# A cached attention kernel: V in one buffer, K in two, and loops of one unit

## The chip, the cores and the metric

The kernel runs on one core of a Trainium2 chip. TensorE (PE), VectorE (DVE), ScalarE (ACT), GpSimd (POOL) and SyncE (SP) each work through an instruction list of their own and wait for each other by semaphores. SP issues all loads; 16 DMA engines carry them out. The metric is the device time of one execution in microseconds. The version before takes 1937.41 us, the median of 3 runs (1937.18 to 1937.42).

## The reference

Two independent attention blocks, A and B, are computed and their outputs put side by side:

```python
def _A_ref(x, k_cache, v_cache, wq, wo):       # B's is the same
    q = (x @ wq).reshape(B, Sq, Hq, Dh).transpose(0, 2, 1, 3)
    scores = jnp.einsum("bhqd,bhkd->bhqk", q, k) * (Dh ** -0.5)
    p = _softmax(scores, axis=-1)
    o = jnp.einsum("bhqk,bhkd->bhqd", p, v)
    return o.transpose(0, 2, 1, 3).reshape(B, Sq, Hq * Dh) @ wo
```

The batch is 2, there is one query row, 32 heads, 8192 cached positions, a head size of 192, and a model size of 640. All is bf16. The caches K and V are by far the largest inputs: each of the four is 2 x 32 x 8192 x 192 numbers, some 201 MB. Every number of them is used once.

## The kernel before

**Units.** A unit u is two neighbouring heads of one batch entry of one block: 64 units, 0 to 63. Its K is one load of 6144 KB, its V another; 128 partitions hold the two heads' positions, 64 partitions for each head and 128 positions for each partition. First the queries are made from x and wq and stand in `qall`, spread over the partitions.

**One unit, step by step.** The names are those of the keys in the code, and the prediction uses them too.
- m(u,c), c = 0 to 3: VectorE multiplies a quarter of K(u) with the query into one of two `prod` buffers (`dve_mul`).
- s(u,c): TensorE adds up the 192 products of a position to 16 partial sums, by 12 matmuls with the identity, into a PSUM bank `scps` (`pe_sum`). m(u,c+2) needs s(u,c) done, as there are two `prod` buffers.
- r(u,c): VectorE adds up the 16 partial sums into `sc` (`dve_red`).
- mx(u): VectorE takes the maximum in each partition (`dve_max`); AR(u): GpSimd takes it over all partitions with a partition all-reduce (`pool_ar`).
- nb(u), exp(u): ScalarE scales the maximum and takes the exponential of `sc` into `pb`, with the sums in `rs` (`act_nb`, `act_exp`).
- l(u), pv(u): TensorE adds up `rs` and multiplies `pb` with V(u) by 64 matmuls into a PSUM bank `ops` (`pe_l`, `pe_pv`).
- rc, oh, os(u): VectorE takes the reciprocal of the sum and adds the two halves of the result; of(u): ScalarE scales and stores it.

At the end the results are turned by small matmuls (`pe_turn`), and multiplied with wo (`pe_out`), which is loaded in pieces into buffers that have come free.

**Buffers and loads.** Three buffers of 128 partitions x 24576 numbers rotate over the sequence K0, K1, V0, K2, V1, K3, V2 and so on, whichever kind a load is. Load number i waits until what load i - 3 brought has been used:

```python
return ("m", u, NCH - 1) if kind == "k" else ("pv", u)   # done(i - 3)
```

So V(u) takes the buffer of K(u), after m(u,3), and K(u+1) that of V(u-2), after pv(u-2). `sc`, `mp`, `mg`, `nb`, `rs`, `rc`, `pb` and `ops` exist three times, `scps` three times.

**Order.** The order of each engine's instructions is written out by hand: `put(engine, slot, order, ...)` sorts by slot and then by order within it. VectorE, in slot u: m0, m1, r0, m2, r1, m3, r2, r3, mx, and then rc, oh, os of unit u-2. TensorE: s0, s1, s2, s3 and then l and pv of unit u-1. ScalarE: nb, exp, and of(u-2). `_Stream` finds a stretch that repeats and makes a loop of it; the loops of VectorE, ScalarE and TensorE hold three units, and SP and GpSimd have none. Unit 0 is an exception: m(1,0) stands in slot 0, ahead of r(0,3) and mx(0).

**The end.** SP issues A's whole wo after s(63,3), 29 rows of B's after pv(62), and the last 19 rows in four pieces after pv(63). A row here is 160 KB.

Of the kernel before, what the change touches and what calls it, by code (L numbers as in the profile page):

```python
# [12 lines left out]
class _Stream:  # L13
    virtual = set()

    def __init__(self, name, sem, reg, first=3):
# [101 lines left out]
def build_kernel(nc, blocks, out):  # L118
# [28 lines left out]
    with ExitStack() as es:  # L147
# [4 lines left out]
        rc = [sb(f"rc{i}", [2, 1], F32) for i in range(3)]  # L152
# [4 lines left out]
        pb = [sb(f"pb{i}", [128, 2 * T], BF16) for i in range(3)]  # L157
        actd = sb("actd", [128, 2], F32)
        xw = sb("xw", [128, NBLK * DC * 128 + D], BF16)
        sc = [sb(f"sc{i}", [128, T], F32) for i in range(3)]  # L160
        mp = [sb(f"mp{i}", [128, 2], F32) for i in range(3)]
        mg = [sb(f"mg{i}", [128, 2], F32) for i in range(3)]
        nb = [sb(f"nb{i}", [128, 1], F32) for i in range(3)]
        rs = [sb(f"rs{i}", [128, 2], F32) for i in range(3)]
# [7 lines left out]
        ops = [ps(f"ops{i}", [128, 512], F32) for i in range(3)]  # L172
        scps = [ps(f"scps{i}", [128, TC, DG], F32) for i in range(3)]
# [3 lines left out]
        oacc = [outps[:], qbank[(LASTU * NCH + 1) % 3]]  # L177
        qps = qbank + [outps[:]]
# [16 lines left out]
        S_pe = _Stream("pe", sem("s_pe"), reg, 1)  # L195
# [24 lines left out]
        bk, b62, b63 = buf["k", LASTU], buf["v", LASTU - 1], buf["v", LASTU]  # L220
        assert (bk, b62, b63) == (2, 0, 1)
        woA, wo0, wo1 = bk * BUFE, b62 * BUFE, b63 * BUFE
        pieces = []
        for blk, rows, off, w in ((0, (WR,), woA, [("s", LASTU, NCH - 1)]), (1, (29,), wo0, [("pv", LASTU - 1)]),
                                  (1, (11, 5, 2, 1), wo1, [("pv", LASTU)])):
            r = 29 if off == wo1 else 0
            for n in rows:
                pieces.append((blk, r, r + n, off, w))
                off, r, w = off + n * D, r + n, []
            assert r == (29 if off == wo0 + 29 * D else WR)  # L230
        NA = 0
        assert 29 * D <= BUFE and woA + WR * D <= NBUF * BUFE + 2 * PRODE
# [21 lines left out]
        def ld_wo(n):  # L254
            blk, r0, r1, off, _ = pieces[n]
            src = blocks[blk]["wo"].rearrange("(p i) n -> p (i n)", i=WR)
            return dma(big[:, off:off + (r1 - r0) * D], src[:, r0 * D:r1 * D], ("wo", n))

        def ld_kv(kind, u):
            hp, b = u // B, u % B  # L260
            blk, h = hp // PPB, 2 * (hp % PPB)
            src = blocks[blk][kind][b, h:h + 2].rearrange("s (p t) d -> (s p) t d", p=64)
            return dma(kv[buf[kind, u]], src, (kind, u))

        def pool_ar(u):
            return lambda eng: eng.partition_all_reduce(mg[u % 3][:], mp[u % 3][:], 128, bass.bass_isa.ReduceOp.max)  # L266
# [21 lines left out]
        def dve_red(u, c):  # L288
            return lambda eng: eng.tensor_reduce(sc[u % 3][:, c * TC:(c + 1) * TC], scps[(u * NCH + c) % 3][:], AXL.X, ALU.add)  # L289

        def dve_max(u):
            def fn(eng):
                for s in range(2):
                    r = slice(64 * s, 64 * s + 64)
                    ins = eng.tensor_reduce(mp[u % 3][r, s:s + 1], sc[u % 3][r, :], AXL.X, ALU.max)  # L295
                return ins
            return fn

        def dve_rc(u):
            return lambda eng: eng.reciprocal(rc[u % 3][:], ops[u % 3][0:2, QW:QW + 1])  # L300

        def dve_ohi(u):
            return lambda eng: eng.tensor_copy(o_hi[:], ops[u % 3][32:34, Dh:QW])  # L303

        def dve_osum(u):
            return lambda eng: eng.tensor_tensor(o_sum[:], ops[u % 3][0:2, 0:Dh], o_hi[:], ALU.add)  # L306

        def act_of(u):
            return lambda eng: eng.activation(qall[0:2, S_act.at(u), :], o_sum[:].unsqueeze(1), ACTF.Identity, scale=rc[u % 3][:])  # L309

        def act_nb(u):
            def fn(eng):
                for s in range(2):
                    r = slice(64 * s, 64 * s + 64)
                    ins = eng.activation(nb[u % 3][r, :], mg[u % 3][r, s:s + 1], ACTF.Identity, scale=-scale)  # L315
# [3 lines left out]
        def act_exp(u):  # L319
            def fn(eng):  # L320
                for s in range(2):
                    r = slice(64 * s, 64 * s + 64)
                    dst = pb[u % 3][r, :].rearrange("p (g a j s) -> p g a j s", a=2, j=JB, s=2)[:, :, :, :, s]
                    ins = eng.activation(dst, sc[u % 3][r, :].rearrange("p (g j a) -> p g a j", j=JB, a=2),  # L324
                                         ACTF.Exp, bias=nb[u % 3][r, :], scale=scale, accum_out=rs[u % 3][r, s:s + 1])
# [33 lines left out]
        def pe_sum(u, c):  # L359
            def fn(eng):  # L360
                for j in range(NJ):
                    ins = eng.matmul(scps[(u * NCH + c) % 3][:], ident[:], prod[c % 2][:, :, j * DG:(j + 1) * DG],  # L362
# [4 lines left out]
        def pe_l(u):  # L367
            return lambda eng: eng.matmul(ops[u % 3][0:2, QW:QW + 1], rs[u % 3][:], ones[:], start=True, stop=True)  # L368

        def pe_pv(u):  # L370
            vv = kv[buf["v", u]].rearrange("p (j a) d -> p j (a d)", a=2)

            def fn(eng):
                for j in range(TJ):
                    j0s = 4 * JB * (j // JB) + 2 * (j % JB)
                    ins = eng.matmul(ops[u % 3][0:MP, 0:QW], pb[u % 3][:, j0s:j0s + MP], vv[:, j, :],  # L376
# [20 lines left out]
        def pe_out(n):  # L397
            blk, r0, r1, off, _ = pieces[n]
            wo = big[:, off:off + (r1 - r0) * D].rearrange("p (i n) -> p i n", n=D)
# [9 lines left out]

        def pe_idle(eng):  # L410
            for i in range(8):
                ins = eng.matmul(ops[(LASTU + 1) % 3][:], ident[:], big[:, woA + 512 * i:woA + 512 * (i + 1)], start=True, stop=True)
            return ins
# [21 lines left out]
        for u in range(NU):  # L435
            for c in range(NCH):
                w = [("k", u), ("pq", NP - 1), ("qa", NP - 1), ("qx", NP - 1), back("s", u, c, 2)]
                slot, order = (0, 9.2) if (u, c) == (1, 0) else (u, 2 + 2 * c)
                put("dve", slot, order, dve_mul(u, c), w, ("m", u, c), ("m", c, u % 3))
                put("dve", u, 5 + 2 * c if c < NCH - 1 else 9.5, dve_red(u, c),  # L440
                    [("s", u, c), key("mx", u - 3), key("exp", u - 3)], ("r", u, c), ("r", c, u % 3))
                put("pe", u, 0.1 * c, pe_sum(u, c),
                    [("m", u, c), ("os", -2) if (u, c) == (1, 0) else None, back("r", u, c, 3), ("id1",), ("qx", NP - 1), ("qa", NP - 1)], ("s", u, c), ("s", c, u % 3))
            put("dve", u, 12, dve_max(u), [("r", u, NCH - 1), key("ar", u - 3), ("init",)], ("mx", u), ("mx", u % 3))
            put("pool", u, 0, pool_ar(u), [("mx", u), key("nb", u - 3)], ("ar", u), ("ar", u % 3))
            put("act", u, 0, act_nb(u), [("ar", u), key("exp", u - 3)], ("nb", u), ("nb", u % 3))
            put("act", u, 1, act_exp(u), [("nb", u), key("pv", u - 3), key("l", u - 3), ("init",)], ("exp", u), ("exp", u % 3))
            w0 = [("exp", u), key("os", u - 3), key("rc", u - 3), ("init",)]
            pslot = u + 1
            pe_o = 2  # L450
            put("pe", pslot, pe_o, pe_l(u), w0, ("l", u), ("l", u % 3))
            put("pe", pslot, pe_o + 0.1, pe_pv(u), [("v", u)], ("pv", u), ("pv", u % 3, buf["v", u]))
            put("dve", u + 2, 20, dve_rc(u), [("pv", u), key("of", u - 3)], ("rc", u), ("rc", u % 3))
            put("dve", u + 2, 21, dve_ohi(u), [("pv", u), key("os", u - 1)], ("oh", u), ("oh", u % 3))
            put("dve", u + 2, 22, dve_osum(u), [("oh", u), key("of", u - 1)], ("os", u), ("os", u % 3))
            put("act", u + 2, 4, act_of(u), [("os", u), ("rc", u)], ("of", u), ("of", u % 3))
# [11 lines left out]
        put("act", NU, 6, act_ot(0), [("t", 1, HQ - 1)], ("ot", 0))  # L468
        put("act", E2, 6, act_ot(1), [("t", 1, HL)], ("ot", 1))
        for n, p in enumerate(pieces):  # L470
# [3 lines left out]
            put("pe", E2, 0.01 * n if n <= NA else 2 + 0.01 * n, pe_out(n), w, ("f", n))  # L474
        put("pe", E2, 1, pe_idle, [("of", LASTU)], None)
# [3 lines left out]

        def done(i):  # L480
            if i < 0:
                return None
            kind, u = loads[i]
            return ("m", u, NCH - 1) if kind == "k" else ("pv", u)
# [22 lines left out]
        fills = [(mp[i], -3.0e38) for i in range(3)] + [(t[i], 0.0) for i in range(3) for t in (rs, pb)]  # L507
        for n, (t, v) in enumerate(fills):
            S_pool.add((lambda t, v: (lambda eng: eng.memset(t[:], v)))(t, v), sig=("init",) if n == len(fills) - 1 else None)
        for n in range(128 // HP):  # L510
# [10 lines left out]
                              ("r", u, 2), ("r", u, 3), ("mx", u), ("rc", u - 2), ("oh", u - 2), ("os", u - 2)],  # L521
# [90 lines left out]
```

## Time and profile before

| | us |
|---|---|
| median of 3 runs | 1937.41 |
| the profiled execution: span | 1936.0 |
| TensorE busy (matmuls) | 1545.0 (80%) |
| VectorE busy | 1124.0 (58%) |
| ScalarE busy | 142.3 (7%) |
| GpSimd busy | 28.4 (1%) |
| moved by DMA | 836.91 MB at 432 GB/s |

The span runs from the first to the last instruction of the profiled execution; the runs are timed from outside. "Idle before" in a group's row is the time in which the engine had nothing to do ahead of such an instruction, with what ended most of it. A DMA issue is a short row on SP's queue (SPq); "us to landing" counts from the issue until the last of the 16 engines has reported. In a timeline, the first number is the start from the beginning of the span, the second the time from the start to the end of the row; rows of equal kind that follow each other are merged, with their count at the end (x24).

### The profile page before, as it was taken

The numbers are of one execution on the slowest core, as the hardware profiler recorded it, in microseconds if no ns is written. First come the engines' busy times: TensorE is split into PE (matmuls) and PEld (weight loads), VectorE is DVE, ScalarE is ACT, GpSimd is POOL, SyncE is SP. The second block draws the span as 40 slices with busy tenths as digits, with TensorE's granted clock in tenths as the row PEclk, the third lists the DMA queues.
The fourth block names the chain that finished last, engine by engine and source line by source line (L and its number), as shares of the span: only waits on it lengthen the run. The fifth ranks groups of instructions, "written<-read, shape, count | busy, mean of one in ns | idle before, by whom it ended". The sixth has DMA issues, their size and how long they took to land.

```text
span 1936.0 us, 19059 instructions
## 1 busy us (share of the span) xinstructions
PE 1545.0 (80%) x7728; PEld 743.0 (38%) x7729; DVE 1124.0 (58%) x907; ACT 142.3 (7%) x519; POOL 28.4 (1%) x113
## 2 busy tenths in 40 slices
PE   5777878878878878878878878878878878878878
PEld 2333434434434434434434434433433433433434
DVE  4765565565565565565565565565565565565560
ACT  3100000000000000000000000000000000000000
POOL 0000000000000000000000000000000000000000
PEclk9899989988989988989988999999999999999999
DMA  9999999999999999999999999999999999999999
GB/s 419 427 435 436 432 434 438 430 434 437 434 433 434 437 431 435 437 432 433 436 436 431 434 438 429 436 437 432 434 435 436 430 436 438 428 436 437 433 433 391
DMA packets 19610, 836.91 MB, mean 432 GB/s; under 512 B 2184, under 2 KB 2320, under 8 KB 2576
## 3 DMA queue, kind: packets, MB, share of 16 engines
q1 hardware_dynamic: 19600, 836.78, 99.9%
q8 instruction: 6, 0.10, 0.0%
q14 instruction: 4, 0.03, 0.0%
HBM read 836.77 MB, written 0.01 MB: 432 GB/s over the span
## 4 chain that ended last, share of the span: by engine, by line
DMA 49%; PE 31%; DVE 17%; issue 3%; DVEq 0%; SPq 0%; ACT 0%; ACTq 0%
DMA big<-in_B_k_cache_dram 24%; DMA big<-in_A_k_cache_dram 22%; PE ops L376 18%; DVE big L285 15%; PE scps L362 12%; DMA big<-in_B_wq_dram 2%; DVE sc L289 1%; DMA big<-in_B_wo_dram 1%; PE scps L354 0%; PE ops L368 0%; PE outps L354 0%; DVEq L285 0%; DVE qall L275 0%; PE scps L404 0%; PE oTps L390 0%
## 5 line engine op out<-in xcount | busy, mean ns | idle before, releaser
L285 DVE TENSOR_TENSOR big<-big,qall 128x6144 bf16<-128x6144 bf16 x256 | 852.7, 3351 | 490.7 <-DMA big<-in_B_k_cache_dram 260.6
L362 PE MATMUL scps<-big,ident 128*128 128x512 bf16 x3072 | 815.6, 426 | 358.2 <-DVE big L285 355.7
L376 PE MATMUL ops<-big,pb 128*34 128x384 bf16 x4096 | 676.8, 326 | 0.0
L362 PEld LDWEIGHTS scps<-big,ident 128*128 128x128 bf16 x3072 | 314.3, 107 | 852.7 <-DVE big L285 439.2
L376 PEld LDWEIGHTS ops<-big,pb 128*34 128x34 bf16 x4096 | 395.5, 98 | 258.7
L289 DVE TENSOR_REDUCE sc<-scps 128x32 f32<-128x512 f32 x256 | 175.9, 687 | 227.7 <-PE scps L362 227.7
L315 ACT ACTIVATE nb<-mg 64x1 f32<-64x1 f32 x128 | 25.8, 201 | 1707.7 <-POOL mg L266 1706.9
L324 ACT ACTIVATE pb<-sc,nb 64x128 bf16<-64x128 f32 x128 | 55.8, 436 | 7.8
L266 POOL PARTITION_ALL_REDUCE mg<-mp x64 | 25.7, 402 | 1859.1 <-DVE mp L295 1859.1
L295 DVE TENSOR_REDUCE mp<-sc 64x1 f32<-64x128 f32 x128 | 35.9, 280 | 8.3
L309 ACT ACTIVATE qall<-o_sum,rc 2x192 f32 (+1 forms) x64 | 29.0, 453 | 20.7 <-DVE o_sum L306 19.1
L306 DVE TENSOR_TENSOR o_sum<-ops,o_hi 2x192 f32<-2x192 f32 x64 | 22.1, 346 | 7.7
L354 PE MATMUL scps<-big,xw 128*128 x120 | 23.2, 351 | 2.6 <-DVE xw L271 2.2
L324 ACT ACTIVATION_READ_ACCUMULATOR pb<-sc,nb 64x1 f32 x128 | 23.7, 185 | 0.0
L303 DVE COPY o_hi<-ops 2x192 f32<-2x192 f32 x64 | 22.3, 349 | 2.0
L300 DVE RECIPROCAL rc<-ops 2x1 f32<-2x1 f32 x64 | 10.0, 156 | 21.3 <-PE ops L376 19.3
L275 DVE CAST qall<-scps 64x192 f32 x48 | 17.0, 355 | 7.2 <-PE scps L354 5.4
L280 ACT ACTIVATE qall<-scps 64x192 f32 x48 | 15.6, 324 | 30.5 <-DVE qall L275 28.2
L345 PE MATMUL oTps<-ident,xw 4*128 4x4 bf16 x5 | 0.4, 178 | 21.5 <-DMA xw<-in_B_x_dram 21.5
L354 PEld LDWEIGHTS scps<-big,xw 128*128 128x128 bf16 x120 | 12.4, 103 | 12.1 <-issue 5.9
L368 PEld LDWEIGHTS ops<-ones,rs 128*2 128x2 f32 x128 | 5.5, 82 | 26.9 <-issue 26.9
L404 PE MATMUL outps<-big,oT 128*2 128x320 bf16 x96 | 9.2, 369 | 4.6 <-DMA big<-in_A_wo_dram 4.6
(36 smaller groups left out, 67.6 us busy)
## 6 DMA issues: line engine op xcount, KB each, us to landing
big<-in_A_k_cache_dram SPq DMA_DIRECT2D x32, 6144.0 KB, 28.6
big<-in_A_v_cache_dram SPq DMA_DIRECT2D x32, 6144.0 KB, 27.6
big<-in_B_k_cache_dram SPq DMA_DIRECT2D x32, 6144.0 KB, 28.9
big<-in_B_v_cache_dram SPq DMA_DIRECT2D x32, 6144.0 KB, 27.8
big<-in_A_wq_dram SPq DMA_DIRECT2D x1, 7680.0 KB, 21.2
big<-in_B_wq_dram SPq DMA_DIRECT2D x1, 7680.0 KB, 38.2
big<-in_A_wo_dram SPq DMA_DIRECT2D x1, 7680.0 KB, 29.0
big<-in_B_wo_dram SPq DMA_DIRECT2D x1, 4640.0 KB, 29.3
```

What stands on the lines that cost most here:

```text
L266: return lambda eng: eng.partition_all_reduce(mg[u % 3][:], mp[u % 3][:], 128, bass.bass_isa.ReduceOp.max)
L285: return lambda eng: eng.tensor_tensor(prod[c % 2], t[:, c * TC:(c + 1) * TC, :], qall[:, S_dve.at(u), :].broadcast_to([128, TC, Dh]), ALU ...
L289: return lambda eng: eng.tensor_reduce(sc[u % 3][:, c * TC:(c + 1) * TC], scps[(u * NCH + c) % 3][:], AXL.X, ALU.add)
L295: ins = eng.tensor_reduce(mp[u % 3][r, s:s + 1], sc[u % 3][r, :], AXL.X, ALU.max)
L303: return lambda eng: eng.tensor_copy(o_hi[:], ops[u % 3][32:34, Dh:QW])
L306: return lambda eng: eng.tensor_tensor(o_sum[:], ops[u % 3][0:2, 0:Dh], o_hi[:], ALU.add)
L309: return lambda eng: eng.activation(qall[0:2, S_act.at(u), :], o_sum[:].unsqueeze(1), ACTF.Identity, scale=rc[u % 3][:])
L315: ins = eng.activation(nb[u % 3][r, :], mg[u % 3][r, s:s + 1], ACTF.Identity, scale=-scale)
L324: ins = eng.activation(dst, sc[u % 3][r, :].rearrange("p (g j a) -> p g a j", j=JB, a=2), ACTF.Exp, bias=nb[u % 3][r, :], scale=scale, acc ...
L354: ins = eng.matmul(qps[hp % NQ][:, 0:QW], xbc[:, blk, c, :], wq_t[blk][:, c, S_pe.at(off, QW, QW)], start=(c == 0), stop=(c == DC - 1))
L362: ins = eng.matmul(scps[(u * NCH + c) % 3][:], ident[:], prod[c % 2][:, :, j * DG:(j + 1) * DG], start=(j == 0), stop=(j == NJ - 1))
L376: ins = eng.matmul(ops[u % 3][0:MP, 0:QW], pb[u % 3][:, j0s:j0s + MP], vv[:, j, :], start=(j == 0), stop=(j == TJ - 1))
```

## The change

1. Buffers: V has buffer 2 for itself, K alternates between 0 and 1. V(u) waits for pv(u-1), K(u) for m(u-2,3). SP's order stays K(u+1), V(u), K(u+2), V(u+1).
2. `sc`, `mp`, `mg`, `nb`, `rs`, `rc`, `pb` and `ops` exist once; `scps` four times, one bank for each quarter. So r(u,c) waits for exp(u-1), exp(u) for pv(u-1), and l(u) for os(u-1).
3. Order. TensorE: s0, s1, s2, l and pv of unit u-1, and then s3. VectorE: m(u+1,0) of the next unit comes ahead of r(u,3) and mx(u), in every unit, and rc, oh, os(u-1) ahead of that. ScalarE: of(u-1), nb, exp.
4. Loops: one unit on TensorE, ScalarE and GpSimd, two on VectorE and SP.
5. `pool_ar` has a one-element product on GpSimd ahead of the all-reduce. In the built program a library reload stands ahead of each of the two, in every turn of the loop; before, there was one reload, ahead of the first all-reduce.
6. wo: 38 of A's 48 rows are loaded between V(62) and V(63), into K's buffer 0, after m(62,3). The other 10, and 28 of B's, come after m(63,3) and s(63,3), 19 more go into the `prod` buffers, and the last row into `xw`. `pe_idle` is gone.

```diff
-        rc = [sb(f"rc{i}", [2, 1], F32) for i in range(3)]
+        rc = sb("rc", [2, 1], F32)
...
-        ops = [ps(f"ops{i}", [128, 512], F32) for i in range(3)]
-        scps = [ps(f"scps{i}", [128, TC, DG], F32) for i in range(3)]
+        ops = ps("ops", [128, 512], F32)
+        scps = [ps(f"scps{i}", [128, TC, DG], F32) for i in range(NCH)]
...
+        VB = NBUF - 1
...
-            buf[kind, u] = i % NBUF
-            bcount[i % NBUF] += 1
-            reg[(kind, u)] = (bsem[i % NBUF], 16 * bcount[i % NBUF])
+            n = VB if kind == "v" else u % VB
+            buf[kind, u] = n
+            bcount[n] += 1
+            reg[(kind, u)] = (bsem[n], 16 * bcount[n])
...
-        for blk, rows, off, w in ((0, (WR,), woA, [("s", LASTU, NCH - 1)]), (1, (29,), wo0, [("pv", LASTU - 1)]),
-                                  (1, (11, 5, 2, 1), wo1, [("pv", LASTU)])):
+        for blk, rows, t, off, w in ((0, (38, 10), BIG, 0, FREE0), (1, (28,), BIG, WR * D, FREE1),
+                                     (1, (12, 5, 2), BIG, PROD, []), (1, (1,), XW, 0, [])):
...
         def pool_ar(u):
-            return lambda eng: eng.partition_all_reduce(mg[u % 3][:], mp[u % 3][:], 128, bass.bass_isa.ReduceOp.max)
+            def fn(eng):
+                eng.tensor_tensor(pooled[:], ones[:], ones[:], ALU.mult)
+                return eng.partition_all_reduce(mg[:], mp[:], 128, bass.bass_isa.ReduceOp.max)
+            return fn
...
-                slot, order = (0, 9.2) if (u, c) == (1, 0) else (u, 2 + 2 * c)
-                put("dve", slot, order, dve_mul(u, c), w, ("m", u, c), ("m", c, u % 3))
+                put("dve", u if c else u - 1, 2 + 2 * c if c else 9.3, dve_mul(u, c), w, ("m", u, c), ("m", c, u % VB))
                 put("dve", u, 5 + 2 * c if c < NCH - 1 else 9.5, dve_red(u, c),
-                    [("s", u, c), key("mx", u - 3), key("exp", u - 3)], ("r", u, c), ("r", c, u % 3))
-                put("pe", u, 0.1 * c, pe_sum(u, c),
-                    [("m", u, c), ("os", -2) if (u, c) == (1, 0) else None, back("r", u, c, 3), ("id1",), ("qx", NP - 1), ("qa", NP - 1)], ("s", u, c), ("s", c, u % 3))
+                    [("s", u, c), key("exp", u - 1)], ("r", u, c), ("r", c))
+                put("pe", u, 0.1 * c if c < NCH - 1 else 3, pe_sum(u, c),
+                    [("m", u, c), back("r", u, c, NCH), ("id1",), ("qx", NP - 1), ("qa", NP - 1)], ("s", u, c), ("s", c))
...
-            put("dve", u + 2, 20, dve_rc(u), [("pv", u), key("of", u - 3)], ("rc", u), ("rc", u % 3))
+            put("dve", u + 1, 9.20, dve_rc(u), [("pv", u), key("of", u - 1)], ("rc", u), ("rc",))
...
-        for i, (kind, u) in enumerate(loads):
-            w = [done(i - NBUF)]
-            if i in (1, 2):
-                w = [("pq", PPB * i - 1)]
-            S_sp.add(ld_kv(kind, u), waits=w)
-        for n in range(len(pieces)):
+        for kind, u in loads[:-1]:
+            if kind == "k":
+                load(kind, u, [("pq", PPB - 1)] if u == 1 else [key("m", u - VB, NCH - 1)] if u else [])
+            else:
+                load(kind, u, [key("pv", u - 1)] if u else [("pq", NP - 1)])
+        S_sp.add(ld_wo(0), waits=pieces[0][4])
+        load("v", LASTU, [("pv", LASTU - 1)])
+        for n in range(1, len(pieces)):
             S_sp.add(ld_wo(n), waits=pieces[n][4])
```

More of the change, by code (lines that the diff above doesn't have):

```diff
@@ L367, in pe_l @@
         def pe_l(u):
-            return lambda eng: eng.matmul(ops[u % 3][0:2, QW:QW + 1], rs[u % 3][:], ones[:], start=True, stop=True)
+            return lambda eng: eng.matmul(ops[0:2, QW:QW + 1], rs[:], ones[:], start=True, stop=True)
         def pe_pv(u):
@@ L408, in pe_out @@
             return fn
[L410 to L413, printed above, removed]
         NSLOT = NU + 8
@@ L489, in build_kernel, with load @@
         S_sp.add(ld_wq(1))
-        for i, (kind, u) in enumerate(loads):
-            w = [done(i - NBUF)]
-            if i in (1, 2):
-                w = [("pq", PPB * i - 1)]
-            S_sp.add(ld_kv(kind, u), waits=w)
-        for n in range(len(pieces)):
+        def load(kind, u, w):
+            slot = u if kind == "k" else u + 1
+            blk = u // UPB
+            S_sp.add(ld_kv(kind, u), waits=w, tag=(slot, (kind, u % B, blk)))
+        for kind, u in loads[:-1]:
[6 more added lines that the diff above has]
+        for n in range(1, len(pieces)):
             S_sp.add(ld_wo(n), waits=pieces[n][4])
@@ L506, in build_kernel @@
         S_pool.add(lambda eng: eng.memset(ones[:], 1.0))
[L507 removed]
+        fills = [(mp, -3.0e38), (rs, 0.0), (pb, 0.0)]
         for n, (t, v) in enumerate(fills):
```

134 lines of the change are left out of this document (66 added, 68 removed).

## The prediction

> **What bounds the kernel now.** I read the page first: span, DMA queue, groups, issues.
>
> ```profile
> span 1936.0 us, 19059 instructions
> ...
> q1 hardware_dynamic: 19600, 836.78, 99.9%
> ...
> L285 DVE TENSOR_TENSOR big<-big,qall 128x6144 bf16<-128x6144 bf16 x256 | 852.7, 3351 | 490.7 <-DMA big<-in_B_k_cache_dram 260.6
> L362 PE MATMUL scps<-big,ident 128*128 128x512 bf16 x3072 | 815.6, 426 | 358.2 <-DVE big L285 355.7
> ...
> big<-in_A_k_cache_dram SPq DMA_DIRECT2D x32, 6144.0 KB, 28.6
> ...
> big<-in_A_wq_dram SPq DMA_DIRECT2D x1, 7680.0 KB, 21.2
> ```
>
> The queue is busy for 99.9% of the span; VectorE and TensorE wait for loads or for each other. A load takes 28.6 us to land, and the next rows show that moving it takes about half of that. These are the timelines of one unit, by engine: VectorE, TensorE, then SP.
>
> ```profile
> 911.00 6.63 DVE L285 TENSOR_TENSOR big<-big,qall 128x6144 bf16<-128x6144 bf16 x2 [7.96 <-DMA big<-in_A_k_cache_dram]
> 919.75 0.69 DVE L289 TENSOR_REDUCE sc<-scps 128x32 f32<-128x512 f32 x1 [2.13 <-PE scps L362]
> ...
> 940.03 6.63 DVE L285 TENSOR_TENSOR big<-big,qall 128x6144 bf16<-128x6144 bf16 x2 [7.17 <-DMA big<-in_A_k_cache_dram]
> ```
> ```profile
> 914.41 8.30 PE L362 MATMUL scps<-big,ident 128*128 128x512 bf16 x24 [3.21 <-DVE big L285]
> 923.76 2.76 PE L362 MATMUL scps<-big,ident 128*128 128x512 bf16 x12 [1.05 <-DVE big L285]
> 927.63 2.76 PE L362 MATMUL scps<-big,ident 128*128 128x512 bf16 x12 [1.10 <-DVE big L285]
> 930.32 0.19 PE L368 MATMUL ops<-ones,rs 128*2 128x1 f32 x2
> 930.45 10.57 PE L376 MATMUL ops<-big,pb 128*34 128x384 bf16 x64
> 943.44 1.93 PE L362 MATMUL scps<-big,ident 128*128 128x512 bf16 x6 [2.42 <-DVE big L285]
> ```
> ```profile
> 927.60 0.33 SPq L245 DMA_DIRECT2D big<-in_A_v_cache_dram  x1
> 941.05 0.33 SPq L245 DMA_DIRECT2D big<-in_B_k_cache_dram  x1
> ```
>
> K(u) landed at 911.00, K(u+1) at 940.03: 29.03 us for two loads, 14.5 each. V was issued at 927.60, some 12 us before the load ahead of it was through, K at 941.05, with a whole load still ahead. So the queue never runs dry, and a unit costs its bytes, 29.03 us. That reserve of 12 to 14 us is what the change touches. The profiled execution is the span, 1936.0; the median of the runs is 1937.41, so I add 1.4 at the end.
>
> **The change, part by part.** Buffers and SP's order. V(u) now waits for the V product of unit u-1 (pv(u-1)) instead of the last product of unit u (m(u,3), over at 927.58). K(u+2) still waits for m(u,3) only, but stands behind V(u) on SP. So both loads of a unit are issued at the end of pv(u-1), and the reserve is whatever is left between that end and the landing of K(u+1).
>
> TensorE's order: pv(u-1) moves ahead of the fourth sums s(u,3), which gives it 2.7 us (927.63 to 930.32). VectorE's order: m(u+1,0) moves ahead of r(u,3) and the maximum mx(u). So mx(u) now follows the landing of K(u+1). Behind it stand AR(u) on GpSimd, the exponential exp(u), and, since there is one sc, r(u+1,0), which must wait for exp(u). The queue behind r(u+1,0) is m(u+1,2), s(u+1,2), pv(u), and with it V(u+1) and K(u+3). This is the new chain. The old kernel ran its first unit in just this order:
>
> ```profile
> 72.44 3.35 DVE L285 TENSOR_TENSOR big<-big,qall 128x6144 bf16<-128x6144 bf16 x1
> 75.71 0.68 DVE L289 TENSOR_REDUCE sc<-scps 128x32 f32<-128x512 f32 x1
> 76.42 0.57 DVE L295 TENSOR_REDUCE mp<-sc 64x1 f32<-64x128 f32 x2
> 77.03 3.36 DVE L285 TENSOR_TENSOR big<-big,qall 128x6144 bf16<-128x6144 bf16 x1
> ```
>
> GpSimd's rows of that unit and of one later, and the end of ScalarE's exponential:
>
> ```profile
> 77.18 3.42 POOL L266 PARTITION_ALL_REDUCE mg<-mp  x1 [73.94 <-DVE mp L295]
> ...
> 931.91 0.35 POOL L266 PARTITION_ALL_REDUCE mg<-mp  x1 [29.47 <-DVE mp L295]
> ```
> ```profile
> 81.90 0.18 ACT L324 ACTIVATION_READ_ACCUMULATOR pb<-sc,nb 64x1 f32 x1
> ```
>
> Here m(1,0), r(0,3), mx(0), m(1,1) follow each other, and AR took 3.42 us, against 0.35 later, when VectorE has no large product beside it. It ended at 80.60, just after m(1,1) ended at 80.39. Two readings fit: GpSimd is held while the product runs, or the first call after a library load is slow. In the changed kernel both conditions hold in every unit, so either reading charges it.
> The Trainium skill (SBUF — State Buffer, Who interferes with whom) says that a VectorE instruction with two SBUF inputs shuts out a GpSimd instruction that reads SBUF until it ends; by that rule the first reading is the right one, the trace agrees (3.42 beside 0.35), and the sum stays as it is.
>
> From the start of m(u,0), then: to m(u,1), 77.03 - 72.44 = 4.59. To the end of AR(u-1), 80.60 - 77.03 = 3.57. The added one-element GpSimd product: nothing at the least, one AR (0.35) at the most; I take 0.3. AR to the end of exp, 82.08 - 80.60 = 1.48. From r(u,0) to the end of s(u,2), 926.52 - 919.75 = 6.77. To the end of pv, 941.02 - 930.32 = 10.70. Sum 27.41; SP's start 0.03 later: 27.44.
>
> TensorE's clock comes on top, since there is now a pause of about 3.5 us (r(u,0) and m(u,2) after exp) ahead of s(u,2). What such a pause does, by two stretches of stages (PE busy first, granted clock third from the end) and one row of TensorE:
>
> ```profile
> 910.20:913.60 3.40, 1.00 (x7) 0.39 (x4) 2.60 (x1) 0.00 (x0) 0.00 (x0) 1.00 1.03 448
> 913.60:917.00 3.40, 2.59 (x7) 0.94 (x8) 3.40 (x2) 0.00 (x0) 0.00 (x0) 0.50 1.07 463
> ```
> ```profile
> 1842.40 6.83 PE L362 MATMUL scps<-big,ident 128*128 128x512 bf16 x24 [3.53 <-DVE big L285]
> ```
>
> After 3.21 us of pause the granted clock was 0.50, and two sums took 8.30 instead of twice 2.76: 2.8 us lost; after 3.53 us they took 6.83: 1.3 lost. Here the loss falls on s(u,2) and pv, on the chain. Bounds 0 (no stretch that long falls into one clock step) and 2.8; I take 1.7, nearer the lower row, whose pause is like ours. Together 29.1 from m(u,0) to the issue.
>
> The queue's side. How long an issue into a drained queue takes to land beyond its bytes: the first load, 7680 KB, took 21.2; at 14.5 per 6144 KB its bytes are 18.1, so 3.1 over. Two loads: 29.0 + 3.1, and 0.2, my estimate, from a landing to VectorE's start: 32.3. So m(u+2,0) comes 29.1 + 32.3 = 61.4 after m(u,0), 30.7 a unit instead of 29.03. VectorE's own round is shorter: 29.1 and about 1 us for the three small reads of pv, ahead of m(u+1,0), 30.1 in all, so the queue sets the pace.
>
> The run: m(1,0) starts at 72.44 as before; m(3,0) at 72.44 + 61.4 = 133.8; 30 such steps later m(63,0) at 1975.8. Before, m(63,0), the last 36 us (granted clock, DMA share and GB/s at the end of the row) and the last piece of wo:
>
> ```profile
> 1868.01 6.63 DVE L285 TENSOR_TENSOR big<-big,qall 128x6144 bf16<-128x6144 bf16 x2 [8.23 <-DMA big<-in_B_k_cache_dram]
> ```
> ```profile
> 1900.00:1936.00 36.00, 27.25 (x258) 14.81 (x257) 1.81 (x5) 1.56 (x4) 0.00 (x0) 0.91 0.86 370
> ```
> ```profile
> big<-in_B_wo_dram SPq DMA_DIRECT2D x1, 160.0 KB, 23.2
> ```
>
> The end. V(63) is issued at 1975.8 + 29.1 = 2004.9. The 38 rows of A's wo (6080 KB, 14.3 us) stand between V(62) and V(63) and fill the place of a K load, so no further hole. Behind V(63) come 58 rows, 9280 KB, 21.9 us: the last lands at 2004.9 + 3.1 + 14.5 + 21.9 = 2044.4. The old kernel's last piece, issued at about 1910.7, landed 23.2 later, 2.1 before the end: 2046.5, with 1.4 more **2048**. The old end left 14% of 36 us of queue unused, 5 us, so a better order of wo can't be worth more than that.
>
> What I cost at nothing: loop branches of one unit on VectorE, TensorE and ScalarE (on VectorE the loop turns between mx and m(u,1), which waits for nothing else; AR's 3.57 covers it, and if that cover goes, r(u,0) still waits for s(u,0)); K's own two buffers; single rc, nb, rs, ops (their readers end before the next writer in this order); SP's and GpSimd's loops (SP's own work is one row of 0.33 a load); four banks of scps instead of three; wo's last row in xw.
>
> **Not shown: the library load.** In the built program GpSimd gets a library reload ahead of the added product and another ahead of AR, in every unit; before there was one in the whole run, with 73.94 us of idle time after it. The nearest row bounds one: AR after a load took 3.42, without 0.35, so 0 to 3.07, two 0 to 6.14. I take 0, as AR began 77.18 - 76.99 = 0.19 us after mx, and the 3.42 are explained by the product beside it.
>
> **Rivals.** (a) Not slower: AR's 3.42 was once only. Then exp(u-1) is over at 4.59 + 0.1 + 0.3 + 0.35 + 1.48 = 6.8 after m(u,0), r(u,0) waits for s(u,0) or m(u,1) alone (8.1 to 8.75), and the issue comes at 25.6 to 26.25. The round is (25.6 + 32.3) / 2 = 28.95: the bytes still decide. Only the first step costs, m(3,0) at 72.44 + 57.9 = 130.3 instead of 1868.01 - 60 x 29.0 = 128: 1936 + 2 + 1.4 = 1939. It turns at r(u,0) 8.3 after m(u,0); at 8.75 the round is 29.27, 0.24 x 62 = 15 slower. For it: TensorE's pause ahead of s(u,0) shrinks below 3.2, as s(u-1,3) follows pv. Against: 3.42, in just this order.
> (b) The clock holds: without the 1.7 the round is 59.7, m(63,0) at 72.44 + 59.7 x 31 = 1923, the end 68.9 later with V's issue at 27.44: 1993.5. For it: pauses of 1 us (923.76) cost nothing, and clock steps can split a pause; against: all pauses above 2.4 us cost.
> (c) The reloads count 3.07 each. From mx on: 0.1 + 3.07 + 0.3 + 3.07 + 0.35, AR ends 11.45 after m(u,0) instead of 8.46. VectorE's round becomes 30.1 + 3.0 = 33.1, with the full clock loss 34.2: 62 x 4.1 to 62 x 5.2 more, 2195 to 2265. Against it: nothing that the trace shows; it lies in the dark of those 73.94 us.
> The Trainium skill (GPSIMD Engine Reference, Instruction dispatch) gives 5.95 us for loading code at the first call after a reload; by that the estimate is 8.7 us more in the chain and about 2580. No run here shows it, and it is the case that speaks most against this change.
> (d) The reloads cost more than 3.07 each. At twice that, VectorE's round is 33.1 + 6.1 = 39.2 and the time about 2570; for and against as in (c), and against it that AR began 0.19 us after mx.
>
> **How the numbers follow.** The forecast, with 2020 to 2100 about it: 0.38. (b), 1985 to 2019: 0.17. (a): 0.10, of which 0.02 faster (up to 5 us from the end), 0.05 same, 0.03 slightly slower. (c), to 2265: 0.19. (d): 0.16. The range takes in all but (d) and the fastest corner: 1938 to 2265. Within 0.2%, 3.9 us, is what a measurement of this kernel can't tell from no change. Faster 0.02, same 0.05, slower 0.93.
>
> **What will show it.** Right: DMA share clearly below 99.9%; SP waiting for the V product alone; AR's mean near 3.5, or 0.35 after a late added product; r(u,0) waiting for exp, not for sums; m(u,0) every 30.7 us; half clock in s(u,2). Wrong: gaps between mx and AR of several us (reload); a queue still at 99%.

## The result, and the profile after

The changed kernel takes 3209.6 us (median of 4 runs, 3203.4 to 3217.3) beside 1937.3 for the kernel before on the same chip: a ratio of 1.657 (95% interval 1.654 to 1.660). The direction was as predicted, the size was not: 3209.6 lies far above 2048 and above the range's end of 2265. Nearest was rival (d), reloads that cost more than 3.07 us each, and it too was too small at 2570.

From the page of the kernel after: the span, the load queue, the chain that ended last, and four groups (group rows: number, busy time and mean ns of one, then the idle time before them and what ended most of it).

```profile
span 3215.7 us, 20311 instructions
...
q1 hardware_dynamic: 19744, 836.78, 62.4%
...
issue 46%; PE 31%; DVE 20%; ACT 2%; POOL 1%; DVEq 0%; ACTq 0%; POOLq 0%
...
L292 DVE TENSOR_TENSOR big<-big,qall 128x6144 bf16<-128x6144 bf16 x256 | 857.1, 3348 | 3.0 <-ACT qall L287 1.0
...
L296 DVE TENSOR_REDUCE sc<-scps 128x32 f32<-128x512 f32 x256 | 175.4, 685 | 1377.7 <-ACT pb L331 1306.7
...
L271 POOL TENSOR_TENSOR pooled<-ones 128x1 f32<-128x1 f32 x64 | 14.9, 233 | 2471.3 <-issue 2371.3
...
L272 POOL PARTITION_ALL_REDUCE mg<-mp x64 | 23.7, 370 | 672.3 <-issue 672.3
```

The queue is no longer the bound (62.4% where it was 99.9%), and VectorE's products don't wait for K at all (3.0 us in the whole run; 490.7 before). VectorE waits 1306.7 us for exp instead. The all-reduce itself takes 0.37 us, but GpSimd stands idle for 672.3 us ahead of the 64 all-reduces, 10.5 us each, with "issue" as the cause: there is no semaphore that it waits for. That is the library reload. Timeline and groups have no row for it, and its time can only be read as this idle time; where it starts is shown by the short rows MODIFY_POOL_CONFIG of GpSimd's sequencer (POOLq), two for each reload, which the view of a source line lists (count, then ns min/median/max):

```profile
L271 POOLq MODIFY_POOL_CONFIG  x128: 1/11/83, 2.6 to 3148.3; - x128
...
L272 POOLq MODIFY_POOL_CONFIG  x128: 1/1/11, 81.3 to 3173.6; - x128
```

Those for the product stand 0.23 us behind the end of mx (median; in the first and the last unit alone they stand ahead of it), and those for the all-reduce right behind the product. One unit in the timeline (start, duration, engine):

```profile
1538.05 3.34 DVE L292 TENSOR_TENSOR big<-big,qall 128x6144 bf16<-128x6144 bf16 x1
...
1542.10 0.57 DVE L302 TENSOR_REDUCE mp<-sc 64x1 f32<-64x128 f32 x2
...
1554.21 0.18 POOL L271 TENSOR_TENSOR pooled<-ones 128x1 f32<-128x1 f32 x1 [38.07 <-issue]
1565.40 0.37 POOL L272 PARTITION_ALL_REDUCE mg<-mp  x1 [11.01 <-issue]
...
1567.45 0.69 DVE L296 TENSOR_REDUCE sc<-scps 128x32 f32<-128x512 f32 x1 [21.38 <-ACT pb L331]
...
1571.46 5.30 PE L369 MATMUL scps<-big,ident 128*128 128x512 bf16 x12 [22.57 <-DVE big L292]
...
1576.81 10.65 PE L383 MATMUL ops<-big,pb 128*34 128x384 bf16 x64
...
1587.49 0.34 SPq L266 DMA_DIRECT2D big<-in_A_v_cache_dram  x1
...
1588.34 3.33 DVE L292 TENSOR_TENSOR big<-big,qall 128x6144 bf16<-128x6144 bf16 x1
```

mx is over at 1542.67. The product comes 11.5 us later, the all-reduce 11.0 us after that; over the 64 units the means are 11.2 and 10.5. Behind it everything waits in the order that the prediction names: exp, r(u,0), s(u,2), pv. What closes the round is not V's load, though: VectorE has rc, oh and os of pv ahead of the next m(u,0), and starts that at 1588.34, without a wait for K. The unit takes 50.3 us here, 49.3 in the mean.

### The profile page after: what moved, and what is told of

It reads as the page before. It is cut to its first block, busy times and chain, and to the rows that moved or that the text cites. A ratio compares the mean times of both kernels' runs of the same rounds, so it can differ in the third digit from the quotient of the medians.

```text
span 3215.7 us, 20311 instructions
## 1 busy us (share of the span) xinstructions
PE 1565.4 (49%) x7721; PEld 739.3 (23%) x7721; DVE 1123.8 (35%) x907; ACT 141.9 (4%) x519; POOL 40.7 (1%) x171
## 3 DMA queue, kind: packets, MB, share of 16 engines
q1 hardware_dynamic: 19744, 836.78, 62.4%
## 4 chain that ended last, share of the span: by engine, by line
issue 46%; PE 31%; DVE 20%; ACT 2%; POOL 1%; DVEq 0%; ACTq 0%; POOLq 0%
PE ops L383 21%; DVE big L292 17%; PE scps L369 9%; DVE sc L296 1%; ACT pb L331 1%; POOL mg L272 1%; DVE o_hi L310 1%; DVE mp L302 1%; ACT nb L322 1%; POOL pooled L271 0%; PE outps L411 0%; DVEq L110 0%; PE ops L375 0%; PE scps L411 0%; ACTq L110 0%
## 5 line engine op out<-in xcount | busy, mean ns | idle before, releaser
L369 PE MATMUL scps<-big,ident 128*128 128x512 bf16 x3072 | 840.6, 432 | 1609.7 <-DVE big L292 1609.7
L296 DVE TENSOR_REDUCE sc<-scps 128x32 f32<-128x512 f32 x256 | 175.4, 685 | 1377.7 <-ACT pb L331 1306.7
L316 ACT ACTIVATE qall<-o_sum,rc 2x192 f32 x64 | 29.0, 454 | 1318.8 <-DVE o_sum L313 1318.8
L271 POOL TENSOR_TENSOR pooled<-ones 128x1 f32<-128x1 f32 x64 | 14.9, 233 | 2471.3 <-issue 2371.3
L272 POOL PARTITION_ALL_REDUCE mg<-mp x64 | 23.7, 370 | 672.3 <-issue 672.3
L361 PE MATMUL scps<-big,xw 128*128 x160 | 29.1, 349 | 2.2 <-DVE xw L278 2.2
L361 PEld LDWEIGHTS scps<-big,xw 128*128 128x128 bf16 x160 | 16.5, 103 | 14.5 <-issue 6.0
## 6 DMA issues: line engine op xcount, KB each, us to landing
big<-in_A_wo_dram SPq DMA_DIRECT2D x1, 6080.0 KB, 32.2
```

The costliest lines, as they stand in the source:

```text
L272: return eng.partition_all_reduce(mg[:], mp[:], 128, bass.bass_isa.ReduceOp.max)
L296: return lambda eng: eng.tensor_reduce(sc[:, c * TC:(c + 1) * TC], scps[c][:], AXL.X, ALU.add)
L361: ins = eng.matmul(qps[hp % NQ][:, 0:QW], xbc[:, blk, c, :], wq_t[blk][:, c, S_pe.at(off, QW, QW)], start=(c == 0), stop=(c == DC - 1))
L369: ins = eng.matmul(scps[c][:], ident[:], prod[c % 2][:, :, j * DG:(j + 1) * DG], start=(j == 0), stop=(j == NJ - 1))
```

## Experiments

All ratios are to the kernel before on the same chip, with 95% intervals. "The product" is the one-element product on GpSimd.

**1. The change without the product.** GpSimd's loop is written out, too.

```diff
-                eng.tensor_tensor(pooled[:], ones[:], ones[:], ALU.mult)
                 return eng.partition_all_reduce(mg[:], mp[:], 128, bass.bass_isa.ReduceOp.max)
...
-                S_pool.emit(eng, [(1, NSLOT, 1)])
+                S_pool.emit(eng)
```

> The changed kernel without the one-element GpSimd product, and with GpSimd's 64 all-reduces written out as before, so no library reload is left in the run but the first. Theory (the two reloads, some 11.2 and 10.5 us in each unit, stand on the chain from mx over AR and exp to r(u+1,0)): the unit falls by at least 21 us from 50.3 to what the rest of the change makes it; by the prediction's chain 30.7 us a unit, 2048 us, AR at 3.4 to 3.5 us in every unit since it stands beside m(u,1). Rival (a) of the prediction: AR 0.35, 1939 us. Rival (b), no clock loss in s(u,2) and pv: 1993 us. Rival to the theory (the reload is not the cause, the waits of the single buffers are): well above 2500 us.

Measured: 2038.7 us, 1.052 (1.050 to 1.054). So 1171 of the 1272 us lost are the product's, and the rest of the change costs 101. Rows of one unit, and of the page:

```profile
1028.04 3.36 DVE L291 TENSOR_TENSOR big<-big,qall 128x6144 bf16<-128x6144 bf16 x1 [1.37 <-DMA big<-in_B_k_cache_dram]
...
1032.73 3.36 DVE L291 TENSOR_TENSOR big<-big,qall 128x6144 bf16<-128x6144 bf16 x1
1032.79 3.51 POOL L271 PARTITION_ALL_REDUCE mg<-mp  x1 [27.74 <-DVE mp L301]
...
1037.98 0.69 DVE L295 TENSOR_REDUCE sc<-scps 128x32 f32<-128x512 f32 x1 [1.89 <-ACT pb L330]
...
1041.99 4.09 PE L368 MATMUL scps<-big,ident 128*128 128x512 bf16 x12 [3.09 <-DVE big L291]
...
1046.14 10.58 PE L382 MATMUL ops<-big,pb 128*34 128x384 bf16 x64
...
1056.74 0.33 SPq L266 DMA_DIRECT2D big<-in_B_v_cache_dram  x1
...
1088.40 3.36 DVE L291 TENSOR_TENSOR big<-big,qall 128x6144 bf16<-128x6144 bf16 x1
```
```profile
q1 hardware_dynamic: 19744, 836.78, 96.7%
```

This is the prediction's chain, term by term: the all-reduce held for 3.51 us beside m(u,1), r(u,0) waiting for exp, a pause of 3.09 us ahead of s(u,2) and 4.09 for its 12 matmuls, V's issue 28.7 after m(u,0) (29.1 predicted, 0.3 of it the product), and m(u+2,0) 31.7 after that (32.3). In the mean of the run the two are 28.5 and 32.8. A unit takes 30.67 us in the mean; 30.7 was predicted.

**2. The product back, GpSimd's loop still written out.** In program order the reload for the product then stands ahead of the wait for mx, and only the reload for the all-reduce behind it. The trace shows it: the rows MODIFY_POOL_CONFIG for the product start right behind the all-reduce of the unit before, 26.7 us ahead of the end of mx (median).

```diff
-                S_pool.emit(eng, [(1, NSLOT, 1)])
+                S_pool.emit(eng)
```

> The changed kernel with the product, but GpSimd's loop written out. The number of reloads stays 128; but the reload ahead of the product now stands ahead of the wait for mx(u), and only the one ahead of AR stands behind it. If only a reload behind the wait counts: the product beside m(u,1) 3.35, one reload of 10.5, AR 0.37, so about 41.5 us a unit and 2700 us. If every reload counts wherever it stands: 3210 us, as after. If a reload costs nothing: as the run without the product.

Measured: 2702.0 us, 1.395 (1.392 to 1.398), as expected if only a reload behind the wait counts. GpSimd's rows:

```profile
1019.36 3.35 POOL L271 TENSOR_TENSOR pooled<-ones 128x1 f32<-128x1 f32 x1 [26.89 <-DVE mp L302]
1033.39 0.37 POOL L272 PARTITION_ALL_REDUCE mg<-mp  x1 [10.68 <-issue]
```

Now the product waits for mx and runs at once; one reload, 10.7 us here, is left on the path. With none, one and two reloads behind mx the kernel takes 2039, 2702 and 3210: 663 and 508 us, or 10.7 and 8.2 for each of 62 units (the second is some 3 us cheaper than its 11.2 us of idle time, as the product's hold of 3.2 us beside m(u,1), below, goes with it). A reload ahead of the wait costs no time in the chain. (The product takes 3.35 us here as it falls beside m(u,1), 0.18 where it comes late: the same hold as the all-reduce's.)

**3. The load queue empty in most units.** Does a reload take 11 us by itself, or because its code must get past the loads?

```diff
+            n = T if u < 2 else T // 8
...
-                kv[buf[kind, u]], blocks[blk][kind][b, S_sp.at(h, 2)].rearrange("s (p t) d -> (s p) t d", p=64)).then_inc(s, 16)
+                kv[buf[kind, u]][:, 0:n, :],
+                blocks[blk][kind][b, S_sp.at(h, 2)].rearrange("s (p t) d -> (s p) t d", p=64)[:, 0:n, :]).then_inc(s, 16)
```

> The kernel after, but K and V loads of unit 2 and later bring only 16 of the 128 positions of a partition, so 7/8 of both caches' data is left out of the result. The load queue is then nearly idle, while GpSimd still reloads twice a unit. Theory 1: a reload takes 10 to 11 us because its code waits behind the load packets; alone it takes about 6 us, so a unit is 50.2 - 2 x 5 = 40 us and the time about 2590 us. Theory 2: the reload takes 10 to 11 us by itself, the unit stays near 49 to 50 us and the time near 3180 us. In both the loads themselves no longer stand on the path, as they didn't in the kernel after (V(u) there landed 12 us before exp(u) ended).

Measured, in one run: 2755.9 us, between the two theories. The edit empties the queue less than expected. SP's first loop repeats the load of V(1), which is whole, so every second V of block A still brings all its bytes:

```profile
big<-in_A_v_cache_dram SPq DMA_DIRECT2D x16, 6144.0 KB, 17.8
...
big<-in_A_v_cache_dram SPq DMA_DIRECT2D x16, 768.0 KB, 4.1
```

A unit with an idle queue:

```profile
1971.55 0.57 DVE L304 TENSOR_REDUCE mp<-sc 64x1 f32<-64x128 f32 x2
1979.92 0.18 POOL L273 TENSOR_TENSOR pooled<-ones 128x1 f32<-128x1 f32 x1 [34.93 <-issue]
1986.01 0.37 POOL L274 PARTITION_ALL_REDUCE mg<-mp  x1 [5.90 <-issue]
```

The two reloads take 7.8 and 5.9 us here; over all units in which the queue was idle during them, 7.5 (46 of them) and 6.0 (47). In 16 units of the same run the queue was busy during the first reload, in 15 of them with a whole V, and there it took 11.7. So both theories hold in part: about 6 to 7.5 us are the reload's own, and a busy load queue adds 4 to 5. The sum agrees: the two reloads take 14.35 us in the mean of this run and 21.7 in the changed kernel, and 62 x 7.35 = 456 less than 3210 is 2754. Theory 1 put both at 6 and took all loads as an eighth.

The prediction named one figure for this, from the Trainium skill (GPSIMD Engine Reference, Instruction dispatch): 5.95 us for the first call after a reload. The idle queue's 6.0 ahead of the all-reduce agrees; the reload back, for a plain product, takes 7.5, and beside full loads both are nearly twice the figure.

**4. The kernel before, with the product ahead of each all-reduce.** There is a whole unit of time between mx and pv there, so two reloads should hide.

```diff
+        pooled = sb("pooled", [128, 3], F32)
...
+                eng.tensor_tensor(pooled[:, u % 3:u % 3 + 1], ones[:], ones[:], ALU.mult)
+                return eng.partition_all_reduce(mg[u % 3][:], mp[u % 3][:], 128, bass.bass_isa.ReduceOp.max)
```

> The kernel before with the one-element product ahead of every all-reduce: 128 reloads in a kernel that has 26 us of slack between the end of exp(u) and l(u) (904.0 to 930.3). Theory (a reload costs only the time of the chain it stands on): AR comes 11 to 22 us later, exp(u) still ends before l(u), 1937 us, no change. Rival (a reload also takes the load queue's time or holds another engine): slower, by up to 128 x some us, so 2000 us or more.

Measured: 2062.7 us, 1.065 (1.063 to 1.068). A miss: hidden behind compute, the reloads still cost 125 us. VectorE's largest waits in this run:

```profile
DVE big L289 <- DMA big<-in_B_k_cache_dram: 301.5, 32, 11.0
DVE big L289 <- DMA big<-in_A_k_cache_dram: 284.2, 30, 10.5
```

The exponential isn't the cause: TensorE waits for it once in this run, 2.0 us. Nearly all of VectorE's idle time ahead of its products still ends with a K load, as before, but the loads come later. A load is over when all 16 DMA engines have reported; these are the 16 times for the same K load, before and with the product, from the trace's semaphore events (us):

```
before:   996.15  996.30  996.51  996.59  996.60  996.61  996.69  996.72  996.75  996.89  996.93  997.01  997.54  997.64  997.84  997.87
product: 1044.40 1044.47 1044.48 1044.49 1044.69 1044.77 1044.78 1044.80 1044.82 1044.90 1044.94 1045.02 1047.66 1048.58 1050.83 1057.78
```

Twelve engines are together, and four are late, by 3 to 13 us. Over the first 11 units the last engine falls further and further behind the twelfth, from 1 us to 13; from then on it stays 11 to 16 us behind. In the kernel after, where the queue runs dry in every unit, it is never more than 2.1 us behind.

**5. Two controls for that: products without reloads, and a quarter of the reloads.** The first edit is shown against experiment 4, the second against the kernel before. In the first the all-reduce is replaced by a second product; in the second the product stands in every fourth unit.

```diff
-                return eng.partition_all_reduce(mg[u % 3][:], mp[u % 3][:], 128, bass.bass_isa.ReduceOp.max)
+                return eng.tensor_tensor(mg[u % 3][:], mp[u % 3][:], ones[:].broadcast_to([128, 2]), ALU.mult)
```

> The kernel before with the one-element product on GpSimd, and with a second small product (mp times ones) in place of the partition all-reduce. The maximum over the partitions is left out, each partition keeps its own. No reload is left on GpSimd in the loop. Theory (the reloads take load time in e3_before_product, 2062.7 us): 1937 (1933 to 1941), the products themselves are free. Rival (work on GpSimd slows the loads whatever its kind): 2000 to 2063.

Measured: 1937.4 us, 1.000 (0.999 to 1.001). 128 products and no reload cost nothing: it is the reload that takes load time, not work on GpSimd.

```diff
+                if u % 4 == 3:
+                    eng.tensor_tensor(pooled[:, u % 3:u % 3 + 1], ones[:], ones[:], ALU.mult)
```

> The kernel before with the one-element product ahead of the all-reduce in every fourth unit only, so 32 reloads instead of the 128 of e3_before_product (2062.7 us, 125.4 more than before). Theory 1: each reload takes about 0.98 us from the load queue, which has no idle time to give: 1937.3 + 32 x 0.98 = 1969 (1962 to 1975). Theory 2: the four late DMA engines catch up in the three units between: 1937 to 1945.

Measured: 1955.2 us, 1.009 (1.008 to 1.011): 17.9 us for 32 reloads, 0.56 each. Theory 2 falls, the late engines don't catch up (in the second half of this run the last one is 7 to 11 us behind the twelfth); theory 1 has the sign but not the price, which was 0.98 each with 128. Why the price rises with their number is open.

**6. The rest of the change: the three buffers rotate again.** As in experiment 1, but with the buffers and load waits of before; the single `sc`, `pb` and `ops`, the new order on every engine, and 38 rows of wo ahead of the last V stay.

```diff
-            n = VB if kind == "v" else u % VB
+            n = i % NBUF
...
+        for i, (kind, u) in enumerate(loads):
+            w = [done(i - NBUF)]
...
-                S_sp.emit(eng, [(2, UPB, B), (UPB + 2, LASTU + 1, B)])
+                S_sp.emit(eng)
```

> The kernel after without the one-element product (e1_no_product, 2038.7 us), but the three buffers rotate over K and V as in the kernel before: V(u) waits for m(u,3), K(u+1) for pv(u-2), and SP has no loop. The single sc, pb, ops and the order of the engines' work stay those of the kernel after; 38 rows of wo stay between the last two V. Theory (V's one buffer is the whole loss that e1 shows, as its load can't be issued until pv(u-1) is over): the queue is full again, 1937 (1932 to 1945). Rival (the order and the single sc, pb and ops cost by themselves): 2000 to 2040.

Measured: 1937.4 us, 1.000 (0.999 to 1.001); the queue's share is back:

```profile
q1 hardware_dynamic: 19744, 836.78, 99.9%
```

All 101 us of experiment 1 go with the buffer scheme. That it is V's one buffer, and not K's two, is told by SP's waits in experiment 1: its loads wait for pv 63 times, and for a product of K once.

```profile
SPq L266 <- PE ops L382: 1850.7, 63, 32.0
...
SPq L266 <- DVE big L291: 18.0, 1, 18.0
```

The order, the single small buffers, the four banks and the new end cost nothing by themselves, and gain nothing. The loops of one and two units were not tried by themselves: this kernel has three units in the loops of VectorE and TensorE, and none on SP. In experiment 1 their turns can hardly be seen: m(u,1) starts 0.03 us after mx in every unit, and V is issued 0.03 and 0.19 us after pv in turn.

**7. Two `sc` buffers on top of experiment 1.** r(u,0) then doesn't wait for exp(u-1).

```diff
-        sc = sb("sc", [128, T], F32)
+        sc = [sb(f"sc{i}", [128, T], F32) for i in range(2)]
...
-                    [("s", u, c), key("exp", u - 1)], ("r", u, c), ("r", c))
+                    [("s", u, c), key("exp", u - 2)], ("r", u, c), ("r", c, u % 2))
```

> As the run without the product, and with two sc buffers in turn, so that r(u,0) no longer waits for exp(u-1). Theory (without reloads the chain is AR beside m(u,1), exp, r(u,0), s(u,2), pv, load): r(u,0) waits for s(u,0) or m(u,1) alone, the issue comes 25.6 to 26.3 us after m(u,0), the bytes decide again, 1937 to 1951 us, against 2048 without this. If the single V buffer alone makes the queue run dry: no faster than the run without the product.

Measured: 1995.6 us, 1.031 (1.029 to 1.033), outside what either theory expected. The wait went, and V is issued 26.2 us after m(u,0), as the theory has it. That is 3 to 4 us before the K ahead of it has landed in most units, and 43 us came back, but not all 101: the bytes don't decide yet. In experiment 1 V landed 17.4 us behind the K ahead of it when issued just as that landed, and 15.9 when issued 2 us earlier; here, at 3.5 to 4.2, still 15.2 in the mean, and only the K loads, issued 16 us and more ahead, came at 14.5 in the median. In experiment 6, V issued 6.9 to 9.4 us ahead came at 14.5 every time, too. An earlier issue buys less than its own length, until the reserve is long enough.

**8. s(u,3) back ahead of pv**, on top of experiment 1.

```diff
-                put("pe", u, 0.1 * c if c < NCH - 1 else 3, pe_sum(u, c),
+                put("pe", u, 0.1 * c, pe_sum(u, c),
```

> The kernel after without the one-element product (e1_no_product, 2038.7 us), and with s(u,3) back ahead of l and pv of unit u-1 on TensorE, as in the kernel before; all else as in e1. By the prediction's chain pv then stands behind s(u,3): V's issue comes 2.8 us later (2.76 for the sums, no more, as m(u,3) ends 0.2 us before s(u,2) does). Half of it in the unit: 30.7 + 1.4, the time 2038.7 + 62 x 1.4 = 2125 (2105 to 2145). Rival: what sets the unit isn't this chain (the filler run, where s(u,2) was 1.3 us shorter and the time no lower, speaks for it): 2035 to 2060.

Measured: 2156.9 us, 1.113 (1.111 to 1.115). The sign is the theory's, and pv's place ahead of the fourth sums is worth 118 us to this buffer scheme. The size is not: the unit takes 32.44, 1.8 more instead of 1.4. VectorE's row says why:

```profile
L291 DVE TENSOR_TENSOR big<-big,qall 128x6144 bf16<-128x6144 bf16 x256 | 857.1, 3348 | 3.0 <-ACT qall L286 1.0
```

The products no longer wait for K. What turns now is VectorE's own round, m(u,0) to pv's end to rc, oh and os, which stand ahead of m(u+1,0):

```profile
1075.84 0.15 DVE L306 RECIPROCAL rc<-ops 2x1 f32<-2x1 f32 x1 [12.88 <-PE ops L382]
...
1076.69 3.33 DVE L291 TENSOR_TENSOR big<-big,qall 128x6144 bf16<-128x6144 bf16 x1
```

By the prediction this round is 30.1, with 2.76 for s(u,3) 32.9. I had put half of the delay on the two-unit round of the loads and forgotten the round beside it.

**9. The half clock of s(u,2), and a control.** Ten matmuls into a spare PSUM bank fill TensorE's pause ahead of s(u,2), on top of experiment 1; in the control they fill the pause ahead of s(u,0), which isn't on the chain (-0.05 in place of 0.15).

```diff
+            put("pe", u, 0.15, pe_fill, [], ("fill", u), ("fill",))
```

> The kernel after without the one-element product (as in e1_no_product, 2038.7 us), and with ten matmuls of 512 columns into a spare PSUM bank between s(u,1) and s(u,2), about 2.1 us of work in TensorE's pause of 3.09 us there. My step of the prediction: the half clock after that pause lengthens s(u,2) from 2.76 to 4.1 to 4.4 us and lies on the chain to V's issue, half of it in the unit's time. Then s(u,2) is 2.76 again, the unit 30.7 - 0.65 = 30.05, the time 2038.7 - 62 x 0.65 = 1998 (1990 to 2006). Rival: the clock's loss isn't on the path, or the filler itself delays s(u,2): 2035 to 2060.

> A control for e6_filler (2051.0 us): the same ten matmuls a unit, but between s(u-1,3) and s(u,0), where TensorE also pauses for about 3 us and where the chain isn't: r(u,0) waits for exp(u-1), which ends 2 us after s(u,0). The pause ahead of s(u,2), its half clock and the chain stay those of e1_no_product (2038.7 us). Theory 1 (the filler does no harm by itself, and in e6 the wait that follows took the gain): 2039 (2033 to 2046). Theory 2 (the filler by itself makes the loads' holes longer, and in e6 that ate the 40 us that the clock gave back): 2080 to 2100.

Measured: 2051.0 us, 1.057 (1.055 to 1.060), and for the control 2041.4, 1.055 (1.053 to 1.057). The clock did what was expected, the time did not. With the filler:

```profile
1034.10 2.32 PE L376 MATMUL fillps<-ident 128*128 128x512 bf16 x10
...
1037.35 2.76 PE L369 MATMUL scps<-big,ident 128*128 128x512 bf16 x12 [0.94 <-DVE big L292]
...
1040.99 10.58 PE L389 MATMUL ops<-big,pb 128*34 128x384 bf16 x64 [0.75 <-DMA big<-in_A_v_cache_dram]
```

The 12 matmuls of s(u,2) take 2.76 us in every unit, instead of 4.09. But in experiment 1 they take 2.76 in 24 of 62 units, too, and 3.8 in the mean, so there was only 1.0 us to gain, not 1.3. In the mean V is issued 27.7 us after m(u,0) (28.5 in experiment 1), and m(u+2,0) follows 33.9 after that (32.8): the loads took back more than the chain had gained. pv now waits for V in 24 units (21 us in all; 4 units and 5 us in experiment 1). Units of 29.5 and 32.2 us alternate, where V was issued 3.9 and 1.8 us ahead of K's landing and landed 14.5 to 14.7 and 17.5 behind it. The control shows that the same matmuls, placed off the chain, cost no more than 3 us. Why V lands 17.5 behind K here and about 16 in experiment 1, when issued equally early, is open.

## Why the prediction was wrong, step by step

- *"The reload: 0 to 3.07, I take 0."* This step failed. Measured: 11.2 us ahead of the product and 10.5 ahead of the all-reduce. The bound was drawn from the wrong rows: 3.42 and 0.35 are durations of the all-reduce, and a reload lies in the idle time ahead of an instruction, not in its duration. The one reload of the old kernel starts at 3.3 us and lay in 73.94 us of idle time with cause "mx" (its row stands behind this list); this bounds it by 73.94, not by 3.07. That the all-reduce began 0.19 us after mx only says that the reload ahead of it was over by then.
- *The rest of the chain.* With the measured reloads the prediction's own round gives the time: VectorE's 30.1, less 3.1 of the hold, which ends once the all-reduce comes long after m(u,1), and 21.7 for the reloads are 48.7; measured 49.3. The clock's loss makes 0.4 of the difference (s(u,2) takes 4.8 in the mean after its long pause, 4.5 with the prediction's 1.7). It is rival (d)'s mechanism with 11 in place of 6.
- *V's issue waits for pv; 30.7 a unit; 2048.* Right for all but the product: 30.67 and 2038.7 (experiment 1). That the total fits so well is partly luck: the issue came 28.5 after m(u,0), where the prediction has 28.8 without the product's 0.3, and m(u+2,0) 32.8 after the issue, where it has 32.3. Experiment 6 and SP's waits show that the single V buffer is the whole of it.
- *AR held for 3.57 beside m(u,1).* Right: 3.46 in the mean of experiment 1, and 0.37 in the kernel after, "0.35 after a late added product".
- *r(u,0) waits for exp.* Right: 1.89 in experiment 1, 21.38 in the kernel after. Taking it away gives 43 us (experiment 7), where an issue at 26.2 with the prediction's 32.3 behind it would have given 88: m(u+2,0) came 33.5 after the issue, as the loads were still late.
- *Half the clock's loss of 1.7 in each unit; rival (b), 1993.5 without it.* The term was too large. s(u,2) lost 1.3 to 1.7 us in 35 of 62 units of experiment 1 and 2.5 in three, but nothing in 24, 1.0 in the mean; pv lost nothing (10.6). Its price was wrong, too: without it the time is 2051 (experiment 9), as V's landing is late next, which the prediction didn't name.
- *A drained queue costs 3.1, and 0.2 from a landing to VectorE's start.* The first is right for an issue at the landing of the load before (17.4 - 14.5 = 2.9); that an issue 3.5 to 4 us ahead can still cost 0.7 (experiment 7) was missed. The 0.2 had no row behind it; in experiment 1 m(u,0) started 0.15 after the landing that it waited for.
- *VectorE's own round, 30.1, below the queue's 30.7.* Right, and it decides once pv comes later (experiment 8).
- *Costed at nothing: loops, single buffers, four banks, the new end.* Right (experiment 6), for the loops of one and two units only by experiment 1's trace; that wo between the last two V can't be worth more than 5 us, too: it is worth nothing measurable.
- *Rival (a).* Falls with experiment 1: the hold appears in each unit.

The old kernel's reload, from the view of the all-reduce's line:

```profile
L266 POOLq MODIFY_POOL_CONFIG  x2: 1/1/1, 3.3 to 3.3; - x2
```

## What to carry to other kernels

A library reload shows as idle time with cause "issue" ahead of a GpSimd instruction, so bound its price by idle rows and find its start by the rows MODIFY_POOL_CONFIG; look in the built program whether instructions of two libraries alternate in a loop, and if they must, let the reload stand ahead of the semaphore wait. Buffers that let a load be issued only 4 us or less before the one ahead of it has landed can cost queue time even if no engine seems late; 7 us or more cost nothing here. And ahead of pricing a stall on one round, list the other rounds within a few per cent of it: they decide what its removal is worth.

## What the runs showed of the hardware that I had not expected

- A reload takes 6.0 us (to the all-reduce's library) and 7.5 us (back, for a plain product) with an idle load queue, 10.5 and 11.2 beside full loads.
- A reload that is hidden from compute still takes load time: four of 16 DMA engines fall behind, 0.56 us of run time for each of 32 reloads and 0.98 for each of 128. Without another library in between, products on GpSimd cost nothing (1937.4).
- A load issued 3.5 to 4 us before the one ahead of it has landed came 0.7 us late in the mean of experiment 7, and 0.2 in that of experiment 9; what decides it was not found.
